# Rest products of a split hidden transform: 96 weight rows become 128, and the rest's right side is made in column quarters

## The chip, the cores and the metric

The kernel runs on one core of one Trainium2 chip. The metric is the device time of one execution in microseconds, the median of several executions. Before the change it is 716.98 us (three runs, 716.82 to 717.36).

## The reference

Two branches are computed from `x` (2048 x 576 floats) and mixed by a gate. Only the lines that matter are kept:

```python
qkv = (x @ wqkv) ...                      # 32 heads of 18
pq, pk = phi(q), phi(k)                   # where(t > 0, t + 1, exp(t)) + 1e-6
kv  = einsum("bhsd,bhse->bhde", pk, v);  z = einsum("bhsd->bhd", pk)
a_  = (einsum(pq, kv) / (einsum(pq, z) + 1e-6)).reshape(B, S, D) @ wo
# second branch, on the same x
a = einsum("bsd,ed->bse", x, dft_hid_re)
b = einsum("bsd,ed->bse", x, dft_hid_im)
y = einsum("ts,bse->bte", dft_seq_re, a) - einsum("ts,bse->bte", dft_seq_im, b)
g = sigmoid((x * gate_w).sum(-1))
return g * a_ + (1 - g) * y
```

The change concerns the two products over the hidden dimension D = 576, `a` and `b`.

## The kernel before, in words

**Numbers and forms.** Every large product is done in a 32-bit format of TensorE (`fp32r`). A float is split into a high part (`hi_of`, a copy on ScalarE, ACT) and what is left (`lo_of`, a subtraction on VectorE, DVE), and three products are summed: high x high, high x low, low x high.

**Stages in order.** k for 16 row tiles, then k-transposed times x and the small matrix of the attention, then q (the stretch of `q_tile`), then the attention output (L1238), then four stages for the second branch: the hidden product for the real part (`Hidden.run`, L1012), the sequence product for the real part (`sequence`, L1171), the hidden product for the imaginary part (L1012 again), and the sequence product for the imaginary part (L1171 again).

**The hidden product.** Both sides are cut into two by two quarters, and seven products of sums of quarters (the "forms") take the place of eight products of quarters. Half of D is 288 = 128 + 128 + 32 rows. For each of eight pairs `p` of row tiles and each of seven forms `k`, `Hidden.product` issues seven matmuls of 288 columns into one bank: six over the two chunks of 128 rows (three split products each), and one for the *rest*, the last 32 rows. In the rest's matmul the three split products lie stacked: 3 x 32 = 96 rows. Its left side is `xr` (read from the scratch `xrest`: 96 rows a pair), its right side `wl` (read from the scratch `last`). That is 2 x 8 x 7 = 112 rest matmuls among 784.

**Where the forms come from.** `Left` makes the left sides, `right` the right sides, for the real part (`wr`) during the first stages, for the imaginary part (`wi`) between the batches of the first sequence product. `right` has three pieces: two for the chunks of 128 rows and one for the rest. A piece is a generator that does a step at each call: load, two sums, two sums, high part, low part, store to DRAM by GpSimd's queue (POOL). In the rest piece of before, the 32 rows stand three times on 96 partitions, all 288 columns of seven forms wide; the high part is taken on all 96, and rows 32 to 63 are then overwritten by the low part.

**Order.** DVE, ACT and SyncE (SP, which issues the loads) run in the order in which the code is written; from the attention output on, PE (TensorE) does so too. In the q stretch PE's and all along POOL's order is set by a scheduler when the program is built, which weighs the instructions' estimated times; so other instructions on DVE or POOL can change PE's order there. Which step of a rest piece runs when is in two tables: `early` (steps of `wr_pieces[2]` after q tiles 5, 7, 8, 9, 11 and 12) and the tuples in `late` (steps of `wi_pieces[2]` after batches 18, 21, 21, 21, 22 and 22 of the first sequence product). A call on a finished generator does nothing. `late(n)` also issues the loads for the second hidden product: `load_w` (six chunk factors and one rest factor of a form), `load_pair` (four loads for one pair), `load_rest`.

Of the kernel before, what the change touches and what calls it, by code (L numbers as in the profile page):

```python
# [14 lines left out]
P = 128  # L15
# [127 lines left out]
def kernel(  # L143
# [310 lines left out]

    def right(src, rest, order):

        main, last = scratch([P, 7, 2, 2, HALF], "wm"), scratch([96, 7, HALF], "wm")

        def load(k, start):
            c = at(start, [P, 7, 2, HALF], R, "wb")[:P if k < 2 else 96]  # L460
            r, raw = c.bitcast(F)[:, :, 1], src[k] if k < 2 else rest
            for a, b in ((slice(0, 3), slice(0, 3)), (5, 3)):
                begin_after(nc.gpsimd.dma_start(out=r[:, a], in_=raw[:, b]), done[-1])
            return c

        def piece(k, start):

            c = load(k, start)
            r = c.bitcast(F)[:, :, 1]
# [5 lines left out]
            add(r[:, 6], r[:, 4], r[:, 1], ALU.subtract)  # L475
            yield
            hi_of(c[:, :, 0], r)
            yield
            if k < 2:
                for fs in (slice(0, 4), slice(4, 7)):  # L480
                    lo_of(c[:, fs, 1], r[:, fs], c[:, fs, 0])
                    nc.gpsimd.dma_start(out=main[:, fs, k], in_=c.bitcast(F)[:, fs])
                    if fs.start == 0:
                        yield
            else:
                rows = slice(32, 64)
                lo_of(c[rows, :, 0], r[rows], c[rows, :, 0])
                yield
                nc.gpsimd.dma_start(out=last, in_=c.bitcast(F)[:, :, 0])

        return (main, last), [piece(*o) for o in order]

    def go(gen, n=1):
        for _ in range(n):
# [475 lines left out]
    class Hidden:  # L970
# [4 lines left out]
        def load_w(self, k):  # L975
            f, (o, ro) = PRODUCTS[ORDER[k]][1], self.lay.w(k)
            if self.lay.swap:
                wl, rl = at(o, [P, 4, HALF], R, "wf"), at(ro, [P, HALF], R, "wf")
            else:
                wl, rl = rows(o, 4, HALF, R, "wf"), rows(ro, 1, HALF, R, "wf")[:, 0]  # L980
            nc.sync.dma_start(out=wl.bitcast(F), in_=self.main[:, f].rearrange("p c s n -> p (c s) n"))
            nc.sync.dma_start(out=rl.bitcast(F)[:96], in_=self.last[:, f])
            self.w[k] = wl, rl

        def load_rest(self, p):

            self.rest[p] = at(self.lay.rest(p), [P, 7, P], R, "xr")
            n = min(NP * 96 - p * 96, P)
            nc.sync.dma_start(out=self.rest[p].bitcast(F)[:n], in_=xrest[p * 96:p * 96 + n])

        def load_x(self, p, k):

# [14 lines left out]
        def product(self, ps, p, k, start):  # L1007
            x, (w, wl) = self.x[p, k], self.w[k]
            ops = [(x[:, a, c * P:c * P + P], w[:, 2 * c + b]) for c in range(2) for a, b in TURN]
            ops.append((self.rest[p][:96, 6 - k], wl[:96]))  # L1010
            for n, (a, b) in enumerate(ops):
                nc.tensor.matmul(ps, a, b, start=(start and n == 0), stop=(n == len(ops) - 1),  # L1012
                                 skip_group_check=True)
# [258 lines left out]
    def late(n):  # L1272
        for k, parts in enumerate(((1, 5, 5, 5, 9, 9), (10, 13, 13, 13, 17, 17), (18, 21, 21, 21, 22, 22))):
            go(wi_pieces[k], parts.count(n))
        if 24 <= n < 28:
            second.load_w(n - 24)
        if n == 27:
            second.load_rest(0)
        if n == 28:
            second.load_w(4)  # L1280
            second.load_pair(0)
        if n == 29:
            second.load_w(5)
            second.load_w(6)
            second.load_pair(1)
        if n == 30:
            second.load_rest(1)
        if n == 31:
            second.load_pair(2)
            second.load_rest(2)  # L1290
            second.load_rest(4)
            second.load_pair(3)
            second.load_rest(3)
            mi.load(0)
            second.load_pair(4)
            second.load_rest(6)
# [20 lines left out]
def _layouts(inputs):  # L1317
# [27 lines left out]
    def right(w):  # L1345

        main, rest = halves(w)
        quarters = ((0, 0), (1, 0), (1, 1), (0, 1))
        cols = (slice(0, HALF), slice(HALF, D))
        main = np.stack([main[d][:, :, cols[c]] for d, c in quarters], axis=2)  # L1350
        rest = np.stack([rest[d][:, cols[c]] for d, c in quarters], axis=1)
        return main, np.concatenate([rest] * 3)

    x = inputs["A_x"][0]
    wr, wr_rest = right(inputs["B_dft_hid_re"].T)
# [39 lines left out]
```

## Time and profile before

| | us |
|---|---|
| median of three runs | 716.98 (716.82 to 717.36) |
| the profiled execution's own time | 717.38 |
| its span, first to last instruction | 715.7 |
| PE busy | 711.6 (99% of the span) |
| DVE busy | 601.1 (84%) |
| ACT busy | 338.5 (47%) |
| POOL busy | 54.9 (8%) |
| first hidden product (starts at 258.40) | 51.52 |
| first sequence product (starts at 309.92) | 175.21 |
| second hidden product (starts at 485.13) | 52.09 |
| second sequence product (starts at 537.22) | 175.23 |

The profile page gives busy time by engine and by group of instructions; PE is the matmul part of TensorE, PEld its weight loads, which overlap the matmuls. A matmul's duration in a group is longer than the distance to the next one, since matmuls are pipelined: what a matmul costs is read from start to start. "Idle before" is time in which the engine had nothing to do, with the name of what released it.

### The profile page before, as it was taken

The page shows a single profiled execution, that of the slowest core. Times are in us where ns is not written, and L with a number is a line of the kernel's source. Part 1 is how long each engine was busy: PE and PEld are TensorE (multiplying, and loading weights), DVE is VectorE, ACT ScalarE, POOL GpSimd, SP SyncE. Part 2 cuts the span into 40 slices and gives each one's busy share as a digit, 9 for nine tenths or more (in the row PEclk, how much of TensorE's full clock was granted, in tenths as well). Part 3 has the DMA queues.
Part 4 walks back from the last instruction along what each step waited for, and adds up shares of the span by engine and source line. Part 5 has one row for each costly group of instructions (what it writes and reads, how often), then busy time and mean ns, then how long its engine had stood idle before and what let it go on. Part 6 is the DMA issues. An engine that isn't in the chain of part 4 may idle for free.

```text
span 715.7 us, 13965 instructions
## 1 busy us (share of the span) xinstructions
PE 711.6 (99%) x5436; PEld 711.1 (99%) x5436; DVE 601.1 (84%) x1020; ACT 338.5 (47%) x587; POOL 54.9 (8%) x94
## 2 busy tenths in 40 slices
PE   9999999999999999999999999999999999999998
PEld 9999999999999999999999999999999999999998
DVE  5699977687999748989999999857889988888885
ACT  5998445677644444553534334323535433343331
POOL 1112200050131110000010000000000000000000
PEclk9999999999999999999999999999999999999999
DMA  7388896874594589753475675789973544454530
GB/s 259 105 280 312 318 303 209 301 213 129 180 368 183 195 307 366 237 184 118 150 257 184 212 254 208 278 312 402 377 260 94 184 132 144 127 181 155 179 131 34
DMA packets 57525, 157.84 MB, mean 221 GB/s; under 512 B 6388, under 2 KB 15668, under 8 KB 56436
## 3 DMA queue, kind: packets, MB, share of 16 engines
q1 hardware_dynamic: 48404, 118.44, 48.9%
q0 software_dynamic: 8768, 38.12, 14.7%
q8 instruction: 43, 0.70, 0.4%
q10 hardware_dynamic: 288, 0.39, 0.2%
q14 instruction: 22, 0.18, 0.1%
HBM read 114.06 MB, written 41.39 MB: 217 GB/s over the span
## 4 chain that ended last, share of the span: by engine, by line
PE 99%; DVE 0%; issue 0%
PE bank L1171 49%; PE bank L226 23%; PE bank L1012 14%; PE bank L725 8%; PE bank L558 2%; PE bank L826 1%; PE bank L252 1%; PE bank L704 0%; PE bank L707 0%; PE bank L827 0%; DVE row L1188 0%
## 5 line engine op out<-in xcount | busy, mean ns | idle before, releaser
L1171 PE MATMUL bank<-fh,c 128*128 128x288 f32 x1792 | 350.7, 293 | 0.0
L1171 PEld LDWEIGHTS bank<-fh,c 128*128 128x128 f32 x1792 | 285.1, 188 | 0.0
L1171 PE MATMUL bank<-fl,c 128*128 128x288 f32 x896 | 262.3, 293 | 0.0
L196 ACT ACTIVATE c<-craw 128x768 fp32r<-128x768 f32 (+2 forms) x148 | 126.9, 900 | 163.6 <-DVE craw L216 154.0
L1171 PEld LDWEIGHTS bank<-fl,c 128*128 128x128 f32 x896 | 168.2, 188 | 0.0
L206 DVE TENSOR_TENSOR c<-craw,c 128x768 fp32r<-128x768 f32 (+3 forms) x148 | 146.1, 1024 | 0.8 <-ACT c L196 0.8
L226 PE MATMUL bank<-wd,xs 128*128 128x288 f32 (+1 forms) x784 | 104.9, 294 | 0.0
L226 PEld LDWEIGHTS bank<-wd,xs 128*128 128x128 f32 x784 | 103.5, 188 | 0.0
L1012 PE MATMUL bank<-wf,xf 128*128 128x288 f32 x588 | 90.8, 294 | 0.0
L1012 PEld LDWEIGHTS bank<-wf,xf 128*128 128x128 f32 x588 | 83.3, 189 | 0.0
L226 PE MATMUL bank<-mw,qs 128*128 128x288 f32 x448 | 60.7, 295 | 0.0
L725 PE MATMUL bank<-pk,c 128*128 128x288 f32 x448 | 60.0, 294 | 0.0
L725 PEld LDWEIGHTS bank<-pk,c 128*128 128x128 f32 x448 | 59.1, 188 | 0.0
L226 PEld LDWEIGHTS bank<-mw,qs 128*128 128x128 f32 x448 | 59.0, 188 | 0.0
L216 DVE TENSOR_TENSOR craw<-craw,craw 128x256 f32<-128x256 f32 x128 | 54.4, 425 | 5.1
L216 DVE TENSOR_TENSOR ys<-bank,ys 128x288 f32<-128x288 f32 x63 | 28.8, 457 | 28.2 <-PE bank L1171 25.7
L216 DVE TENSOR_TENSOR craw<-craw 128x512 f32<-128x512 f32 x64 | 43.9, 687 | 7.6 <-PE bank L1171 3.7
L196 ACT ACTIVATE fh<-fl 128x864 fp32r<-128x864 f32 (+1 forms) x36 | 30.3, 868 | 28.0 <-DVE fl L216 20.0
L395 DVE SCALAR_TENSOR_TENSOR acc<-bank,e 128x288 f32<-128x288 f32 x64 | 28.6, 454 | 16.5 <-ACT e L394 16.3
L206 DVE TENSOR_TENSOR fl<-fl,fh 128x864 fp32r<-128x864 f32 (+1 forms) x36 | 35.4, 988 | 1.6
L1012 PE MATMUL bank<-wf,xr 96*128 96x288 f32 x112 | 33.3, 298 | 0.0
L216 DVE TENSOR_TENSOR fl<-bank,y 128x288 f32<-128x288 f32 x48 | 21.8, 454 | 11.1 <-PE bank L1012 9.6
(106 smaller groups left out, 662.1 us busy)
## 6 DMA issues: line engine op xcount, KB each, us to landing
xf<-xm SPq DMA_DIRECT2D x42, 512.0 KB, 9.2
craw<-in_cr_dram SPq DMA_DIRECT2D x32, 512.0 KB, 3.9
craw<-in_ci_dram SPq DMA_DIRECT2D x32, 512.0 KB, 3.7
xm<-xb POOLq DMA_DIRECT2D x8, 1024.0 KB, 6.6
wf<-wm SPq DMA_DIRECT2D x14, 576.0 KB, 6.4
xraw<-in_xa_dram SPq DMA_DIRECT2D x25, 320.0 KB, 3.5
xr<-xr SPq DMA_DIRECT2D x14, 448.0 KB, 8.5
xm<-xb POOLq DMA_DIRECT2D x8, 768.0 KB, 8.2
```

The costliest lines, as they stand in the source:

```text
L196: return nc.scalar.activation(dst, src, AF.Copy, bias=bias)
L206: nc.vector.tensor_tensor(out=dst, in0=src, in1=hi, op=ALU.subtract)
L216: nc.vector.tensor_tensor(out=dst, in0=a, in1=b, op=op)
L226: nc.tensor.matmul(ps, a, b, start=(n == 0), stop=(n == len(pairs) - 1))
L252: nc.tensor.matmul(warm[:, :136], unit[:, :P], unit, start=True, stop=True)
L395: nc.vector.scalar_tensor_tensor(dst, ps, 0.0, e, op0=ALU.max, op1=ALU.add)
L558: nc.tensor.matmul(ps[i][h], x[:, i_x * P:(i_x + 1) * P], wkt.row(h, j), start=(c == 0 and n == 0), stop=(c == KC and n == 1))
L725: nc.tensor.matmul(ps[h][:, :HALF], t[:, a, k], pk[s][:, b, half(h)], start=(s == 0 and n == 0), stop=(s == NT - 1 and n == len(turn) - 1))
L826: nc.tensor.transpose(mains[i][:, cs], acc[2 * k + i][:, cs], ident)
L1012: nc.tensor.matmul(ps, a, b, start=(start and n == 0), stop=(n == len(ops) - 1), skip_group_check=True)
L1171: nc.tensor.matmul(ps[q], c[x][l > 2][:, l - 3 * (l > 2), k], factors[p](y, f), start=(p == 0 and i == 0), stop=(p == NP - 1 and i == 2))
```

## The change

- In `Hidden.product` the rest's matmul takes all 128 rows of `xr` and of `wl`. Rows 96 to 127 of the left side are the first 32 rows of the next pair's rest (which were loaded before too, and unused); on the right side they are zero. After the last pair stand 32 new zero rows in `xrest`, so the last pair's load is 128 rows and not 96.
- The rest piece of `right` works on a tile whose 128 partitions are four quarters of the columns (72 each) by 32 rows. Sums, high and low part are made once, on [128, 7, 72]. A third part of the tile is set to zero by POOL.
- Four stores (high, low, high, zero) put it together in `last`, now [128, 4 quarters, 7 forms, 72]. For `wr` two more stores write the zero rows of `xrest`.
- The rest piece has four steps where it had six: the four sums are one step, the low part and all stores another. The tables `early` and `late` keep their numbers, so the last calls do nothing, and the low part follows the high part at once (after batch 21, where it was after batch 22).
- `load_w` reads `wl` as 128 rows of four runs of 72 floats (288 bytes) each, where it read 96 rows of one run of 288 floats (1152 bytes).
- In `late`, `load_rest(4)` comes after `load_rest(3)`.

On SP, after the second hidden product's pair 1, the loads stood in this order (`xf` are a pair's loads, `xr` a rest's, `craw` the first batch of the next sequence matrix):

```order
L989 DMA xr_6122<-xr_103 128x896
L995 DMA xf_6166<-xm_97 128x1024
L995 DMA xf_6168<-xm_97 128x1024
L995 DMA xf_6170<-xm_97 128x1024
L995 DMA xf_6172<-xm_97 128x512
L989 DMA xr_6174<-xr_103 128x896
L989 DMA xr_6176<-xr_103 128x896
L995 DMA xf_6178<-xm_98 128x1024
L995 DMA xf_6180<-xm_98 128x1024
L995 DMA xf_6182<-xm_98 128x1024
L995 DMA xf_6184<-xm_98 128x512
L989 DMA xr_6186<-xr_103 128x896
```

and now, with the lines of the new file (L1009 is `load_rest`, L1015 `load_x`):

```order
L1009 DMA xr_6132<-xr_103 128x896
L1015 DMA xf_6176<-xm_97 128x1024
L1015 DMA xf_6178<-xm_97 128x1024
L1015 DMA xf_6180<-xm_97 128x1024
L1015 DMA xf_6182<-xm_97 128x512
L1009 DMA xr_6184<-xr_103 128x896
L1015 DMA xf_6186<-xm_98 128x1024
L1015 DMA xf_6188<-xm_98 128x1024
L1015 DMA xf_6190<-xm_98 128x1024
L1015 DMA xf_6192<-xm_98 128x512
L1009 DMA xr_6194<-xr_103 128x896
L1009 DMA xr_6196<-xr_103 128x896
```

The second of the two neighbouring `xr` loads (the rest of pair 4) has moved behind pair 3 and its rest. The number of loads is the same.

On POOL, ahead of the moves of the attention's small matrix (L886, `mw`), stood before only stores of the second chunk's forms (`wm`):

```order
L482 DMA wm_359<-wb_1516 128x4x576
L482 DMA wm_359<-wb_1516 128x3x576
L886 DMA mw_1722<-mf_1719 112x2x288
L886 DMA mw_1722<-mf_1719 14x2x288
L886 DMA mw_1722<-mf_1719 2x2x288
```

and now the zero parts for `wr` come between (L492 is the memset, L501 the stores to `last`, L507 those to `xrest`, L906 the moves):

```order
L482 DMA wm_359<-wb_1516 128x4x576
L482 DMA wm_359<-wb_1516 128x3x576
L492 MEMSET wb_2112 128x504
L501 DMA wm_360<-wb_2112 4x32x504
L507 DMA xr_103<-wb_2112 32x448 x2
L906 DMA mw_1722<-mf_1719 112x2x288
```

The other three stores to `last` stand further down, where the one store stood before.

On PE the scheduler's order differs in the q stretch alone. Where the first two attention tiles are transposed (`ident` is the identity matrix; `wd`, `xs` are the q product), before:

```order
L226 MATMUL bank<-wd_1307,xs_2303 128x290
L826 MATMUL bank<-ident_76,acc_87 128x128 x4
L226 MATMUL bank<-wd_1424,xs_2303 128x288 x5
L226 MATMUL bank<-wd_1307,xs_2303 128x290 x5
L826 MATMUL bank<-ident_76,acc_87 128x128 x4
L827 MATMUL bank<-ident_76,last_2043 128x128
L226 MATMUL bank<-wd_1424,xs_2350 128x288
```

and now:

```order
L226 MATMUL bank<-wd_1308,xs_2305 128x290
L226 MATMUL bank<-wd_1424,xs_2305 128x288 x5
L226 MATMUL bank<-wd_1307,xs_2305 128x290 x6
L846 MATMUL bank<-ident_76,acc_87 128x128 x8
L847 MATMUL bank<-ident_76,last_2043 128x128
L226 MATMUL bank<-wd_1424,xs_2358 128x288
```

The two groups of four transposes have become one group of eight; the matmuls are the same in number.

The diff, without the lines that only move:

```diff
-    xrest = scratch([NP * 96, 7 * P], "xr")
-    xrest_of = xrest.rearrange("(g q j r) n -> g j r q n", g=2, q=4, j=3)
+    xrest = scratch([NP * 96 + 32, 7 * P], "xr")
+    xrest_of = xrest[:NP * 96].rearrange("(g q j r) n -> g j r q n", g=2, q=4, j=3)
...
     def right(src, rest, order):
-        main, last = scratch([P, 7, 2, 2, HALF], "wm"), scratch([96, 7, HALF], "wm")
+        main, last = scratch([P, 7, 2, 2, HALF], "wm"), scratch([P, 4, 7, HALF // 4], "wm")
...
-            if k < 2:
...
-            else:
-                rows = slice(32, 64)
-                lo_of(c[rows, :, 0], r[rows], c[rows, :, 0])
-                yield
-                nc.gpsimd.dma_start(out=last, in_=c.bitcast(F)[:, :, 0])
-
-        return (main, last), [piece(*o) for o in order]
+        def rest_piece(start):
+
+            c = at(start, [P, 3, 7, HALF // 4], R, "wb")
+            f = c.bitcast(F)
+            r = f[:, 1]
+            load(r, rest)
+            nc.gpsimd.memset(f[:, 2], 0.0)
+            yield
+            for _ in sums(r):
+                pass
+            yield
+            hi_of(c[:, 0], r)
+            yield
+            lo_of(c[:, 1], r, c[:, 0])
+            for k, a in enumerate((0, 1, 0, 2)):
+                nc.gpsimd.dma_start(
+                    out=last[k * 32:k * 32 + 32].rearrange("r q f n -> q r (f n)"),
+                    in_=f[:, a].rearrange("p f n -> p (f n)"))
+            if src is wr:
+                for k in range(2):
+                    cs = slice(k * 7 * P // 2, (k + 1) * 7 * P // 2)
+                    nc.gpsimd.dma_start(out=xrest[NP * 96:, cs], in_=f[:32, 2].rearrange(
+                        "p f n -> p (f n)")[:, :7 * P // 2])
+
+        return (main, last), [piece(*o) if o[0] < 2 else rest_piece(o[1])
+                              for o in order]
...
-            nc.sync.dma_start(out=rl.bitcast(F)[:96], in_=self.last[:, f])
+            nc.sync.dma_start(out=rl.bitcast(F).rearrange("p (q n) -> p q n", q=4),
+                              in_=self.last[:, :, f])
...
-            n = min(NP * 96 - p * 96, P)
-            nc.sync.dma_start(out=self.rest[p].bitcast(F)[:n], in_=xrest[p * 96:p * 96 + n])
+            nc.sync.dma_start(out=self.rest[p].bitcast(F), in_=xrest[p * 96:p * 96 + P])
...
-            ops.append((self.rest[p][:96, 6 - k], wl[:96]))
+            ops.append((self.rest[p][:, 6 - k], wl))
...
             second.load_rest(2)
-            second.load_rest(4)
             second.load_pair(3)
             second.load_rest(3)
+            second.load_rest(4)
```

More of the change, by code (lines that the diff above doesn't have):

```diff
@@ L455, in right, with load, sums @@
     def right(src, rest, order):
-        main, last = scratch([P, 7, 2, 2, HALF], "wm"), scratch([96, 7, HALF], "wm")
-        def load(k, start):
-            c = at(start, [P, 7, 2, HALF], R, "wb")[:P if k < 2 else 96]
-            r, raw = c.bitcast(F)[:, :, 1], src[k] if k < 2 else rest
+        main, last = scratch([P, 7, 2, 2, HALF], "wm"), scratch([P, 4, 7, HALF // 4], "wm")
+        def load(r, raw):
             for a, b in ((slice(0, 3), slice(0, 3)), (5, 3)):
                 begin_after(nc.gpsimd.dma_start(out=r[:, a], in_=raw[:, b]), done[-1])
[L464 to L469, printed above, removed]
-            yield
+        def sums(r):
             add(r[:, 3], r[:, 5], r[:, 0], ALU.subtract)
@@ L475, in piece @@
             add(r[:, 6], r[:, 4], r[:, 1], ALU.subtract)
+        def piece(k, start):
+            c = at(start, [P, 7, 2, HALF], R, "wb")
+            r = c.bitcast(F)[:, :, 1]
+            load(r, src[k])
+            yield
+            yield from sums(r)
             yield
@@ L1351, in right @@
         rest = np.stack([rest[d][:, cols[c]] for d, c in quarters], axis=1)
-        return main, np.concatenate([rest] * 3)
+        rest = rest.reshape(32, 4, 4, HALF // 4).transpose(2, 0, 1, 3)
+        return main, rest.reshape(P, 4, HALF // 4)
     x = inputs["A_x"][0]
```

12 lines of the change are left out of this document (6 added, 6 removed).

## The prediction

> **What bounds the kernel now.** I read the page's first part, then the chain of work that ended last, then PE's rows in the two hidden products.
>
> ```profile
> span 715.7 us, 13965 instructions
> PE 711.6 (99%) x5436; PEld 711.1 (99%) x5436; DVE 601.1 (84%) x1020; ACT 338.5 (47%) x587; POOL 54.9 (8%) x94
> 258.40 51.52 PE bank L1012 x392
> 309.92 175.21 PE bank L1171 x1344
> 485.13 52.09 PE bank L1012 x392
> 537.22 175.23 PE bank L1171 x1344
> ```
>
> PE is the bound: busy 711.6 of 715.7 us, and in the four stages of the second branch (start, length, name, count of matmuls) the chain is PE alone, without a gap. So the change can win only what PE's matmuls themselves cost, and lose what makes PE wait. Per matmul the chain gives 175.21/1344 = 130.4 ns in the sequence product, 51.52/392 = 131.4 ns in the first hidden product and 52.09/392 = 132.9 ns in the second. The surplus is 392 x 1.07 = 0.42 us and 392 x 2.52 = 0.99 us, 1.41 us in all. The next rows are PE's timeline and its groups by shape.
>
> ```profile
> 262.70 0.30 PE L1012 MATMUL bank<-wf,xr 96*128 96x288 f32 x1
> 262.84 0.95 PE L1012 MATMUL bank<-wf,xb 128*128 128x288 f32 x6
> 263.62 0.30 PE L1012 MATMUL bank<-wf,xr 96*128 96x288 f32 x1
> 492.27 0.30 PE L1012 MATMUL bank<-wf,xr 96*128 96x288 f32 x1
> 492.41 0.96 PE L1012 MATMUL bank<-wf,xf 128*128 128x288 f32 x6
> 493.21 0.30 PE L1012 MATMUL bank<-wf,xr 96*128 96x288 f32 x1
> L1012 PE MATMUL bank<-wf,xr 96*128 96x288 f32 x112 | 33.3, 298 | 0.0
> L1012 PE MATMUL bank<-wf,xb 128*128 128x288 f32 x84 | 12.9, 293 | 0.0
> L1012 PE MATMUL bank<-wf,xf 128*128 128x288 f32 x588 | 90.8, 294 | 0.0
> L1012 PEld LDWEIGHTS bank<-wf,xr 96*128 96x128 f32 x112 | 21.1, 188 | 0.0
> L1012 PEld LDWEIGHTS bank<-wf,xb 128*128 128x128 f32 x84 | 11.8, 189 | 0.0
> ```
>
> A group of seven takes 263.62 - 262.70 = 0.92 us in the first product. After the 96-row matmul the next starts 0.14 us later; the six 128-row ones take 0.78, 0.13 each. In the second product a group takes 0.94: 0.14 after the rest, then 0.80. A 96-row matmul itself lasts 298 ns, the 128-row ones beside it 293 to 294. So there is a small price on the 96 rows, 4 to 5 ns each.
>
> **The change, part by part.**
>
> *128 rows (112 matmuls).* The count of matmuls and columns stays. Of what a rest costs more than its neighbours I take 5 ns (298 less 293): 112 x 5 = 0.56 us gained, on the chain. Ends: nothing, if the surplus comes from the change of bank that also falls there; and 1.41 us, if the whole surplus over the sequence product went with it. I stay near the low middle, since in the second product the six full matmuls are slow too (0.80 against 0.78), which the change leaves.
>
> *One group of transposes for two, on PE.*
>
> ```profile
> 182.95 0.60 PE L826 MATMUL bank<-ident,acc 128*128 128x128 f32 x4
> 183.31 1.57 PE L226 MATMUL bank<-wd,xs 128*128 128x288 f32 x10
> 185.18 1.03 PE L226 MATMUL bank<-wd,xs 128*128 128x288 f32 x6
> ```
>
> Ten matmuls at 0.13 us with the last one's 0.29 would last 1.46 us, six 0.94; both rows behind transposes have 0.09 to 0.11 more. One such change falls away: 0.09 us gained; the ends are 0 and 0.2. The first four transposes come about 1.4 us later, but the attention output does not start before all `wd` matmuls of the stretch are through.
>
> *DVE and ACT, rest pieces.*
>
> ```profile
> L216 DVE TENSOR_TENSOR wb<-wb 96x288 f32<-96x288 f32 x8 | 3.5, 450 | 0.1
> L206 DVE TENSOR_TENSOR wb<-wb 32x2016 fp32r<-32x2016 f32 x2 | 4.5, 2248 | 0.1
> L216 DVE TENSOR_TENSOR kvs<-kvs,mask 72x72 f32<-72x72 f32 x1 | 0.2, 228 | 0.0
> L206 DVE TENSOR_TENSOR xs<-xs,xs 128x512 fp32r<-128x512 f32 x4 | 2.8, 693 | 1.2 <-ACT xs L196 1.1
> L196 ACT ACTIVATE xs<-xs 128x512 fp32r<-128x512 f32 x4 | 2.5, 620 | 0.9 <-DMA xs<-in_xf_dram 0.9
> ```
>
> A piece took 4 x 450 + 2248 = 4.05 us of DVE. Now, by the nearest rows, 4 x 228 + 693 = 1.6. Two pieces give DVE about 4.9 us, which buys nothing: no PE group above has idle time ahead of it. The low part now directly follows the high part, so DVE waits for ACT, some 0.6 us after batch 21, with the next batch's sums queued behind. DVE spends 0.9 + 0.6 + 0.7 = 2.2 us there; before, the low part alone put 2.25 us into one batch, and PE never waited. Cost nothing; without that cover it would be the 0.6 us wait.
>
> *POOL.* The new zeros stand ahead of the moves of the small matrix, the other stores ahead of stores that come later.
>
> ```profile
> L254 POOL MEMSET ones_f<- 128x128 f32 x1 | 0.2, 204 | 0.3 <-POOLq L1382 0.3
> 146.25 3.08 POOL L886 DMA_DIRECT2D mw<-mf  x5 [15.65 <-ACT mf L874]
> 183.11 0.83 POOL L489 DMA_DIRECT2D wm<-wb  x1 [20.65 <-ACT xs L196]
> ```
>
> Three issues at 0.83 us and a memset (four times the 128 x 128 one's 0.2 us, an estimate) are 3.3 us in a gap of 15.65; three stores, 2.5 us, fall in one of 20.65. For `wi` it is four stores after batch 21, while the loads that read them begin after batch 24, three batches of 175.21/32 = 5.5 us later. No cost.
>
> *Loads of `wl` (14).* 96 packets of 1152 bytes become 512 of 288. The price of a packet is read from stretches with one size: mean 27 ns at 512 bytes (91.6 to 92.4 us: 16 x 0.8 x 1.142 / 538), 52 ns at 1152 (240 to 240.9: 16 x 0.9 x 1.056 / 294).
>
> ```profile
> DMA packets 538, 0.26 MB, mean 324 GB/s; under 512 B 32, under 2 KB 538, under 8 KB 538
> q1 hardware_dynamic: 538, 0.26, 114.2%
> DMA packets 294, 0.34 MB, mean 376 GB/s; under 512 B 0, under 2 KB 294, under 8 KB 294
> q1 hardware_dynamic: 294, 0.34, 105.6%
> L981 SPq DMA_DIRECT2D wf<-wm x14: 319/370/563, 190.1 to 474.5; - x14
> 473.35 0.69 SPq L982 DMA_DIRECT2D wf<-wm  x1
> 470.00:480.00 10.00, 10.00 (x80) 10.00 (x78) 4.23 (x5) 1.79 (x2) 0.00 (x0) 1.00 0.96 349
> 480.00:490.00 10.00, 10.00 (x79) 10.00 (x77) 5.48 (x11) 1.43 (x4) 0.00 (x0) 1.00 1.03 383
> ```
>
> The line through both gives 18.5 ns at 288 bytes: over 16 engines 0.59 us a load, against 0.31 before. Below that the end is 13 ns (by bytes), above it 52 ns (a packet costs the same whatever its size, 1.66 us a load). The last three loads, for forms 4 to 6 (that for form 5 at 473.35; the last `L981` ahead of form 6's at 474.5), fall where the DMA engines are full (0.96, then 1.03 in the column before the last), so all that follows them is late by 3 x 0.28 = 0.84 us, and at the worst by 3 x 1.35 = 4.1. The tightest of those is the rest of pair 1:
>
> ```profile
> 482.04 0.32 SPq L989 DMA_DIRECT2D xr<-xr  x1
> 487.03 1.63 SPq L989 DMA_DIRECT2D xr<-xr  x2
> 494.54 0.32 SPq L989 DMA_DIRECT2D xr<-xr  x1
> DMA to landing us min/median/max: 8.0/8.3/8.5
> ```
>
> The last row is for the rests issued between 480 and 505 us. Issued at 482.04, it lands by 490.5; PE uses it at 492.27 (above), its weight load a step earlier. That leaves 1.6 us, and 2.1 at a landing of 8.0. At my price PE does not wait. The other rests have more: pair 2's, issued at 487.03, is needed at 485.13 + 2 x 6.51 + 0.8 = 498.9 (a pair takes 52.09/8), pair 3's lands at 503.0 and is needed at 505.5.
>
> *The moved rest of pair 4.* Pair 3's four loads and its rest come a load earlier, about 1.2 us. The moved one goes at about 495 instead of 488, lands by 503.5 and is needed at 485.13 + 4 x 6.51 + 0.8 = 512. No cost.
>
> *The last pair's 32 more rows and the first product's loads.* Less than 0.3 us more for a load with pairs ahead of it; the first product's `wl` loads are issued from 190 us on, for 258.40. No cost.
>
> Sum: -0.56 - 0.09 = -0.65 us. The profiled execution took 717.38 us, 0.40 above the median; it would become 716.7, and the median 716.98 becomes 716.3.
>
> **The rivals.**
>
> *The rows cost nothing.* The 5 ns lie at the change of bank and stay; only 0.09 us are gained: 716.9. For it speaks that a group of seven in which all are full would also change bank there; against it that the sequence product changes bank as well, every sixth matmul, at 130.4 ns a step. The Trainium skill says on its page "TensorE: Matmul & The Clock Gate", section "LDWEIGHTS (loading the stationary operand)", that a weight load of 32 rows takes as long as one of 128, since its columns count; by that rule the sum would be -0.09 us. The trace agrees for the load alone (188 and 189 ns) and shows the matmul of 96 rows 5 ns longer.
>
> *Small packets make PE wait (the other side).* If a packet of 288 bytes costs over 29 ns, the three loads make what follows 1.65 us late and PE stops at pair 1's rest; at 52 ns, 4.1 us less 1.6 to 2.1, some 2.2 us of waiting, once, since later rests then have that much more time: 716.98 + 2.2 - 0.65 = 718.5. For it speaks that no packet of this size is in the trace; against it that 512 bytes cost half of 1152. The Trainium skill, page "DMA: Bandwidth & Descriptors", section "Specifications", asks for 512 bytes at least for full rate and says that below this the engine reads, modifies and writes; if that doubled 18.5 to 37 ns, an estimate, the delay would be 2.6 us and the time 717.1. No run so far shows it.
>
> *The whole surplus goes.* If the row change disturbs the neighbours too, 1.41 + 0.09 us are won: 715.5. Against it: only the step behind the rest stands out in the first product.
>
> **How the numbers follow.** A change under 0.2% (1.43 us) can't be told from none here. Forecast (716.3, from 715.9 to 716.7): 0.60. Rows cost nothing, 716.9: 0.17. Small packets make PE wait: 0.13, half of it below 717.9, half up to 718.6. Whole surplus, 715.5: 0.06. Something else, either way: 0.04. The range from 715.7 to 717.5 holds the first two and the mild half of the third, and leaves out the rest. Only the sharp packets and half of the remainder are slower by over 0.2%: 0.08; faster is part of the whole-surplus case: 0.05; the same 0.87.
>
> **What would show it.** A group of seven of 0.915 us in the first hidden product instead of 0.92, with all seven steps alike, and the stages at about 51.2 and 51.8 us; one row of eight transposes; DVE busy some 5 us less, to no effect. Wrong would be: a PE gap near 492 us ahead of an `xr` matmul (the packets), or stages of 51.5 and 52.1 us still (the rows).

## The result, and the profile after

The changed kernel takes 725.94 us (median of 4 runs, 725.18 to 727.11) against 717.10 for the kernel before (4 runs, 716.82 to 717.36): 1.0124 times, 95% interval 1.0109 to 1.0139. It is 8.8 us slower; 0.65 us less had been forecast. The profiled execution took 725.7 us.

The page's first lines, the engines, and the long pieces of the chain of waits (start, length, what):

```profile
span 723.5 us, 13984 instructions
PE 713.2 (99%) x5436; PEld 711.6 (98%) x5436; DVE 596.1 (82%) x1020; ACT 336.4 (46%) x587; POOL 61.0 (8%) x104
254.23 11.51 DMA wf<-wm
265.88 46.22 PE bank L1032 x339
312.76 142.37 PE bank L1191 x1092
457.93 8.98 DMA craw<-in_cr_dram
482.39 10.98 PE bank L1191 x82
493.37 51.72 PE bank L1032 x392
545.09 175.22 PE bank L1191 x1344
```

PE's busy share is still 99%, and that alone would hide everything. The chain shows it: before, each of the four stages of the second branch was one piece of PE; now a load (`wf<-wm`, a right side's form) breaks the first hidden product, and a load of the sequence matrix (`craw`) breaks the first sequence product. By the stages' borders: the first hidden product ends 312.76 - 309.92 = 2.84 us later; the sequence product takes 493.37 - 312.76 = 180.61 us for 175.21, 5.40 more; the second hidden product 0.37 less, the last stage the same. The sum is 7.86 us of a span that grew by 7.8. There are two losses and one small gain.

**The sequence product.** POOL's timeline (start, duration, what; in brackets the idle time before it and what ended that), then SP's:

```profile
422.14 0.74 POOL L501 DMA_DIRECT2D wm<-wb  x1 [0.42 <-POOL wb L492]
433.25 0.73 POOL L501 DMA_DIRECT2D wm<-wb  x1 [10.37 <-ACT wb L196]
440.32 0.71 POOL L501 DMA_DIRECT2D wm<-wb  x1 [6.34 <-issue]
447.02 0.69 POOL L501 DMA_DIRECT2D wm<-wb  x1 [5.99 <-DVE craw L216]
```

```profile
454.15 0.32 SPq L1001 DMA_DIRECT2D wf<-wm  x1
...
455.15 0.56 SPq L1128 DMA_DIRECT2D craw<-in_cr_dram  x1
457.93 1.66 SPq L1128 DMA_DIRECT2D craw<-in_cr_dram  x1
```

The four stores of `wi`'s rest forms don't go out in a row. The first holds the zeros. The data of the third were ready with the second (433.25), and still it is issued 7.07 us later; "issue" says that nothing the profile records held POOL. The fourth goes 6.70 us after that. Its row names DVE, but the low part that it stores was done at 433.47. What fits is the landing of the store before. From issue to landing the four stores take (least, median, most):

```profile
DMA to landing us min/median/max: 6.4/6.8/8.2
```

The last three land 6.8, 6.4 and 6.8 us after their issue, at about 440.1, 446.7 and 453.8. Each time the next in line, two stores and then SP's load, goes some 0.3 us later. SP's first load of a form for the second hidden product (L1001) stands until 454.15, 7.1 us after the last store was issued. SP works in the order of the code, so the two `craw` loads behind it stand as well. SP's waits (total us, times, longest) from 440 to 490 us now, and from 436 to 470 us before, where that load was issued at 443.65:

```profile
SPq L1001 <- DMA wm<-wb: 8.3, 1, 8.3
```

```profile
SPq L981 <- DMA wm<-wb: 0.7, 1, 0.7
```

The buffer in which the rest piece lies is where the first form's factor goes, so the load has to wait for the last store out of it. What then comes late, on DVE (which waits 7.70 us here) and on PE:

```profile
460.87 0.69 DVE L216 TENSOR_TENSOR craw<-craw 128x512 f32<-128x512 f32 x1 [7.70 <-DMA craw<-in_cr_dram]
460.56 0.29 PE L1191 MATMUL bank<-fh,c 128*128 128x288 f32 x1
463.74 0.40 PE L1191 MATMUL bank<-fh,c 128*128 128x288 f32 x1 [2.90 <-DVE c L206]
```

From 460.56 to 463.74 PE does one matmul. Together with three smaller ones (0.63, 1.26 and 0.41 us behind the matmuls that start at 469.19, 475.27 and 481.98) this is 3.18 + 2.30 = 5.48 us from start to start. Four usual steps of 0.13 us are in it, and the step behind each wait is 0.11 longer than usual (463.74 to 463.98): 5.48 - 0.52 + 0.44 = 5.40, the stage's growth.

**The first hidden product.** PE's timeline, then a table of windows (window, its length, PE busy, granted clock, share of the DMA engines, GB/s):

```profile
262.97 0.95 PE L1032 MATMUL bank<-wf,xb 128*128 128x288 f32 x6
265.88 0.37 PE L1032 MATMUL bank<-wf,xr 128*128 128x288 f32 x1 [1.96 <-DMA wf<-wm]
268.26 0.44 PE L1032 MATMUL bank<-wf,xr 128*128 128x288 f32 x1
269.94 0.44 PE L1032 MATMUL bank<-wf,xr 128*128 128x288 f32 x1
```

```profile
263.60:265.80 2.20, 0.32 (x3) 1.00 1.02 414
265.90:267.00 1.10, 1.10 (x8) 1.00 1.01 413
267.40:270.60 3.20, 3.20 (x15) 0.50 1.03 412
460.90:463.70 2.80, 0.00 (x0) 1.00 1.06 393
463.80:467.00 3.20, 3.20 (x25) 1.00 1.06 403
467.00:470.00 3.00, 2.67 (x21) 1.00 1.02 376
```

The rest's matmul that should follow the six of 262.97 at 263.76 starts at 265.88: it waits 2.1 us for `wl` of form 6, whose load took 11.51 us. Then the granted clock falls to 0.50 and a group takes 269.94 - 268.26 = 1.68 us instead of 0.92. POOL's same instruction (L1261, L1241 before) stands at 258.57 instead of 259.34, so the stage began about 0.77 us earlier and grew by 2.84 + 0.77 = 3.6 us: 2.1 of waiting, about 1.5 of slow clock. Both numbers are this execution's: where the same loads and stores stand in this stage, after_act (below) waits 1.97 us, after_rq 0.91 and after_sooner 0.28, all three with the clock at 1.00.

The two DMA queues while that load ran (257.8 to 259.4 us; packets, MB, share of 16 engines):

```profile
q0 software_dynamic: 79, 0.65, 95.6%
q1 hardware_dynamic: 80, 0.02, 6.0%
```

q0 carries POOL's stores, here 8192 bytes a packet (0.65 MB / 79), q1 SP's loads, 288 bytes a packet. They take turns, 79 to 80. The load has 512 packets, 32 an engine, and for each it waits for a large one, as long as POOL's stores last. At 1.6 x 16 / 79 = 0.32 us for a pair of packets, 32 turns are some 10 us, an estimate; the load took 11.51. The Trainium skill, page "DMA: Bandwidth & Descriptors", section "Queues, rings and completion order", says that an engine goes round its queues packet by packet, and that a packet is some 9 to 17 descriptors; the trace agrees with the turns and has one transfer of 288 bytes in a turn.

### The profile page after: what moved, and what is told of

It reads as the page before. It is cut to its first block, busy times and chain, and to the rows that moved or that the text cites. A ratio compares the mean times of both kernels' runs of the same rounds, so it can differ in the third digit from the quotient of the medians.

```text
span 723.5 us, 13984 instructions
## 1 busy us (share of the span) xinstructions
PE 713.2 (99%) x5436; PEld 711.6 (98%) x5436; DVE 596.1 (82%) x1020; ACT 336.4 (46%) x587; POOL 61.0 (8%) x104
## 4 chain that ended last, share of the span: by engine, by line
PE 88%; issue 4%; DMA 3%; DVE 3%; POOL 1%; SPq 0%; ACT 0%; POOLq 0%; DVEq 0%
PE bank L1191 45%; PE bank L226 17%; PE bank L1032 14%; PE bank L745 8%; PE bank L578 2%; DMA wf<-wm 2%; DMA craw<-in_cr_dram 1%; DVE c L206 1%; POOL att L1261 1%; PE bank L252 1%; DVE craw L216 1%; PE bank L846 0%; PE bank L724 0%; DVE ys L216 0%; DMA att<-acc 0%
## 5 line engine op out<-in xcount | busy, mean ns | idle before, releaser
L1032 PE MATMUL bank<-wf,xr 128*128 128x288 f32 x112 | 33.3, 297 | 2.0 <-DMA wf<-wm 2.0
```

## The experiments

Theory 1: the stores' slowness and the load behind them make the sequence product's 5.4 us. Theory 2: the short packets make the first hidden product's 3.6 us. Rivals: the stores' number, their time, or the 128 rows themselves; and, for theory 2, that the load is merely issued too late. The table gathers all fourteen runs: the ratio to the kernel before on the same chip, lengths of the stages by the chain (a `>` marks a first hidden product that waits inside), and how long after the start of the sequence product SP's load for the first form was issued. The kernel before has 133.7 in the last column.

| kernel | us | ratio | first hidden | sequence | SP's load after |
|---|---|---|---|---|---|
| changed | 725.94 | 1.0124 [1.0109, 1.0139] | >55.1 | 180.61 | 141.4 |
| rows_only | 717.28 | 0.9998 [0.9989, 1.0006] | 51.41 | 175.21 | 134.7 |
| after_act | 719.92 | 1.0036 [1.0022, 1.0050] | > | 175.28 | 137.5 |
| after_early | 723.85 | 1.0099 [1.0084, 1.0115] | 51.34 | 179.21 | 141.0 |
| rows_short | 716.60 | 0.9994 [0.9985, 1.0003] | 51.40 | 175.21 | 134.3 |
| after_long | 722.22 | 1.0068 [1.0054, 1.0081] | 51.42 | 180.51 | 141.9 |
| short_late | 722.15 | 1.0068 [1.0050, 1.0086] | >56.6 | 175.21 | 133.9 |
| only_late | 717.95 | 1.0005 [0.9995, 1.0015] | >52.0 | 175.21 | 134.5 |
| after_both | 717.81 | 1.0010 [1.0001, 1.0019] | 51.51 | 175.21 | 136.2 |
| rows_four | 716.79 | 0.9999 [0.9988, 1.0009] | 51.41 | 175.21 | 133.1 |
| after_sooner | 722.68 | 1.0082 [1.0067, 1.0097] | >51.6 | 181.45 | 141.9 |
| both_unswap | 718.60 | 1.0022 [1.0012, 1.0031] | 51.43 | 176.70 | 137.5 |
| after_rq | 718.83 | 1.0029 [1.0018, 1.0040] | > | 175.21 | 133.1 |
| rows_shape | 735.54 | 1.0258 [1.0239, 1.0277] | 51.40 | 194.66 | 155.6 |
| rq_early | 717.30 | 1.0009 [1.0000, 1.0018] | 51.34 | 175.21 | 133.1 |

The second hidden product is 51.72 or 51.73 us in all of them.

### The 128 rows alone (rows_only)

```diff
 # of the kernel before: one store and loads of 1152 bytes stay
+ nc.gpsimd.memset(full.bitcast(F)[96:, :, 0], 0.0)
...
- nc.sync.dma_start(out=rl.bitcast(F)[:96], in_=self.last[:, f])
+ nc.sync.dma_start(out=rl.bitcast(F), in_=self.last[:, f])
...
- ops.append((self.rest[p][:96, 6 - k], wl[:96]))
+ ops.append((self.rest[p][:, 6 - k], wl))
```

> The 128 rows alone: the kernel before, with the rest piece made on 96 partitions as before, 32 zero rows below it, one store of the rest's right side, and its loads as 128 runs of 1152 bytes. Theory: the rows themselves gain, the loss is all in how the rest's right side is stored and loaded. The trace of the changed kernel shows groups of seven of 0.912 us where they were 0.920, 8 ns for each rest: 112 x 8 = 0.9 us gained, 716.1 us, both hidden products at about 51.1 and 51.7 us, no idle time on PE. Rival: the 128 rows cost something by themselves (more to load, another order on PE): 717.5 or more.

Measured: 717.28 us, like the kernel before. The stages are shorter (chain):

```profile
258.49 51.41 PE bank L1018 x392
...
485.10 51.72 PE bank L1018 x392
```

That is 0.11 + 0.37 = 0.48 us less on PE than before. The interval of the total, -0.8 to +0.4 us, holds this and also nothing: the total expected wasn't seen. What follows is that the rows are not where the loss is.

### The stores on another queue (after_act)

```diff
-                nc.gpsimd.dma_start(
+                (nc.scalar if src is wi else nc.gpsimd).dma_start(
                     out=last[k * 32:k * 32 + 32].rearrange("r q f n -> q r (f n)"),
```

> The changed kernel, with the four stores of the imaginary part's rest forms issued by ACT instead of POOL. Theory 1: on POOL each of these stores waits for the one before it to land (6 to 7 us each), the buffer they read comes free some 10 us late, the first factor load of the second hidden product waits for it at the head of SP's queue, and the sequence matrix's batches behind it are late. Then the first sequence product returns from 180.6 to about 175.3 us, and the time from 725.9 to about 720.6. Rival: the batches are late because the loads of 288-byte runs stand ahead of them among the DMA packets; then the sequence product stays at 179 us or more and the time above 724.

Measured: the sequence product is back, the first hidden product still waits.

```profile
266.88 45.31 PE bank L1032 x344
312.19 175.28 PE bank L1191 x1344
```

SP's load goes at 449.73, 137.5 us after the stage's start and 3.9 earlier than in the changed kernel, and that is enough. Theory 1 holds as far as the queue: on ACT's queue the four stores are issued in 3.86 us, and the same data in the same shape cost the stage nothing.

### The load of form 6 earlier (after_early)

```diff
+            if not self.lay.swap and k == 6:
+                rl = self.early          # loaded by load_last(6)
...
+        if i == 13:
+            hidden.load_last(6)
```

> The changed kernel, with the last rest factor of the first hidden product (form 6) loaded after attention tile 13 instead of 14, before POOL's last stores of left forms start. Theory 2: its 512 packets of 288 bytes took turns with POOL's packets of 8192 and 6144 bytes, one for one, and so took 8 us to pass instead of about 1; PE waited 2.1 us for it and then ran some 3 us at half the granted clock. Then the first hidden product returns from 55.1 to about 51.1 us and the time from 725.9 to about 722. Rival: the stretch simply holds too many bytes; then pairs or factors behind are late, the product stays above 53 us, and the time above 724.

Measured: the first hidden product is one piece again, 51.34 us; the sequence product is not (PE's timeline holds a wait of 2.80 us for DVE at 459.95).

```profile
257.72 51.34 PE bank L1042 x392
309.06 142.37 PE bank L1201 x1092
```

The total gains only 2.1 us (725.94 - 723.85). The runs spread: 720.59 for the profiled one, whose mean granted clock is 1.000, and 723.75 to 725.46 for three with 0.995. A mean of 0.995 is 1% of the time at 0.50, some 7 us in which PE does 3.6 us of work less, an estimate that fits the 3.2 to 4.9 us between them. So the same gaps probably cost more in those three, the clock falling behind them; only the first was profiled.

### Short packets without the rest of the change (rows_short)

The load of `wl` in rows_only in runs of 72 floats; the elements are other than those the product needs.

```diff
-            nc.sync.dma_start(out=rl.bitcast(F), in_=self.last[:, f])
+            nc.sync.dma_start(out=rl.bitcast(F).rearrange("p (q n) -> p q n", q=4),
+                              in_=self.last[:, min(f, 3):min(f, 3) + 4, :HALF // 4])
```

> The 128-row kernel with one store (rows_only), but the rest factors loaded as 512 runs of 288 bytes (a quarter of four neighbouring forms each, so the rest products use other elements than they should). Only the loads' packets differ from rows_only. Theory 2: the first hidden product is about 4 us longer than in rows_only by a wait for form 6's rest factor and the clock behind it, the first sequence product is not, and the time is about 720. Rival (the piece's stores are the whole loss, packets cost only their 19 ns): 716.2, as rows_only. Third: the short runs hurt both places, 724 or more.

Measured: no wait, 51.40 us. Theory 2's expectation is missed. Why, the DMA queues from 257.6 to 258.2 us show:

```profile
q1 hardware_dynamic: 302, 0.09, 80.6%
q0 software_dynamic: 1, 0.01, 3.2%
```

Here the short packets ran before POOL's large ones had begun; there was nothing to take turns with. So shortness alone isn't the cause; theory 2 became: short packets *behind* POOL's large ones. The next three kernels test this.

### Long runs in the changed kernel (after_long)

Here, and in short_late below, the rest products again use other elements than they should.

```diff
-            nc.sync.dma_start(out=rl.bitcast(F).rearrange("p (q n) -> p q n", q=4),
-                              in_=self.last[:, :, f])
+            nc.sync.dma_start(out=rl.bitcast(F), in_=self.last.rearrange(
+                "r q f n -> r (q f n)")[:, f * HALF:(f + 1) * HALF])
```

> The changed kernel, its stores as they are, but a rest factor is loaded as 128 runs of 1152 bytes, each 288 floats in a row of the stored rest forms (so the rest products use elements of other forms). Only the loads' packets differ from the changed kernel. Theory 2: the wait in the first hidden product goes (about 51.4 us instead of 55.1); the first sequence product keeps its 5 us from the stores on POOL (theory 1): about 722. Rival for the sequence: if the short packets ahead of the matrix's batches count for some of it, it falls below 179 us too.

Measured: the first hidden product is whole, the sequence product keeps its loss (51.42 and 490.41 - 309.90 = 180.51 us by the chain). In the profiles the load that is early or long never makes PE wait in the first hidden product (after_early, after_long, after_both, both_unswap, rq_early), and the one that is neither always does (changed, after_act, after_rq, after_sooner).

### The same place, short and long (short_late, only_late)

These are rows_short and rows_only with form 6's `wl` loaded behind the rest of pair 3, 0.7 to 0.8 us later:

```diff
+            if self.lay.swap or k < 6:
+                self.load_last(k)
...
+        if i == 15:
+            hidden.load_last(6)
```

> The 128-row kernel with rest factors as 512 runs of 288 bytes (rows_short), and with form 6's rest factor loaded one transfer later, behind pair 3's rest of 448 KB. In rows_short its packets went out just ahead of POOL's 8192-byte ones, in the changed kernel just behind the first of them. If taking turns one for one is the mechanism, 32 short packets an engine now need some 8 us: PE waits 2 to 5 us in the first hidden product (54 to 58 us instead of 51.4), the time is 719.5 to 723. Rival (the changed kernel's wait came from something else in its stores or its POOL order): no wait, 716.6 to 717.3.

> The control for short_late: the 128-row kernel with rest factors as 128 runs of 1152 bytes (rows_only), form 6's loaded one transfer later in the same way. If packets take turns, 8 packets an engine need some 3 us where 32 need 8: the product stays at 51.4 us or waits under 1 us, 717 to 718. Rival (bytes or the place in the queue decide, not the number of packets): as late as short_late.

PE's timelines, short_late first:

```profile
263.41 0.95 PE L1025 MATMUL bank<-wf,xb 128*128 128x288 f32 x6
267.99 0.58 PE L1025 MATMUL bank<-wf,xr 128*128 128x288 f32 x1 [3.64 <-DMA wf<-wm]
268.37 1.64 PE L1025 MATMUL bank<-wf,xb 128*128 128x288 f32 x6
```

```profile
264.00 0.95 PE L1024 MATMUL bank<-wf,xb 128*128 128x288 f32 x6
265.23 0.37 PE L1024 MATMUL bank<-wf,xr 128*128 128x288 f32 x1 [0.28 <-DMA wf<-wm]
```

At the same place the 512 packets of 288 bytes make PE stop for 3.64 us and the 128 of 1152 bytes for 0.28, although the bytes are the same. The loss is 4.9 us (722.15; two runs) against 0.7 (717.95). In short_late the clock also falls to 0.50 behind the wait (268 to 270 us). This shows theory 2 in its second form, and that lateness alone costs little.

### Both undone (after_both)

after_act and after_early together.

```diff
+                (nc.scalar if src is wi else nc.gpsimd).dma_start(
...
+            hidden.load_last(6)
```

> The changed kernel with both remedies: the imaginary part's stores on ACT's queue, and form 6's rest factor loaded after attention tile 13. If the two places are the whole loss, the hidden products take 51.4 and 51.7 us, the sequence products 175.2, and the time is 716.2 to 716.9, the same as before or 0.1% less. If more is lost elsewhere, above 718.

Measured: 717.81 us. Both stages are whole in the chain (51.51 and 175.21 us), and 8.1 of the 8.8 us are gone. The time is 0.9 us above the range expected; no stage of the profiled execution (716.94 us) shows where.

### Four stores of another shape (rows_four), and sooner (after_sooner)

rows_four is rows_only with `wi`'s one store cut into four of 32 partitions; after_sooner is the changed kernel with the rest piece's last steps a batch earlier.

```diff
+ for q in range(4):
+     qs = slice(q * 32, q * 32 + 32)
+     nc.gpsimd.dma_start(out=last[qs], in_=full.bitcast(F)[qs, :, 0])
```

```diff
- (18, 21, 21, 21, 22, 22)
+ (18, 20, 20, 20)
```

> The 128-row kernel (rows_only) with the imaginary part's single store of rest forms cut into four stores of 32 rows each on POOL, nothing else. Theory 1 alone: each store waits for the one before it, 5 to 7 us each, so the buffer comes free 15 to 20 us later than in rows_only, SP's first factor load stands that long, the sequence matrix's batches behind it come late, and the first sequence product grows from 175.2 by 10 us or more: 726 or above. Rival (the serial waiting belongs to the 4 x 32 x 504 shape or to the 288-byte loads, not to several stores in a row): 717 to 718.

> The changed kernel, with the imaginary part's rest piece finished after batch 20 of the first sequence product instead of 21, so its chain of stores starts 5.5 us sooner and the factor load waits some 5 us instead of 10.5. Theory 1: the batches behind then come in time or nearly; the first sequence product falls from 180.6 to between 175.2 and 176.5 us, the time by 4 to 5.4 us to about 721. Rival (the sequence's loss is not a matter of when the stores end): no change, 725 to 726.

Four stores cost nothing here; POOL issues two at once and the next as soon as DVE is through:

```profile
431.57 1.14 POOL L495 DMA_DIRECT2D wm<-wb  x2 [12.26 <-ACT wb L196]
435.62 0.56 POOL L495 DMA_DIRECT2D wm<-wb  x1 [2.90 <-DVE wb L206]
```

So it isn't the number of stores. after_sooner missed too: its data are ready sooner, but the four stores stand 7.8 to 9.0 us apart (419.33, 428.21, 435.98, 445.00), each behind the landing of the one before, and SP's load is no earlier in its stage (141.9 us after its start; 141.4). Its sequence product takes 181.45 us, part of it at a clock of 0.50 (461 to 467 us). The time alone would mislead here: 722.68 is 3.3 us under the changed kernel, but in the profiled execution (723.88) what is shorter is the first hidden product (51.6 us against 55.1), which the edit doesn't touch and which waits only 0.28 us here. Finishing the piece a batch sooner bought the sequence product nothing. What is left is the stores' shape.

### The shape (after_rq, rows_shape)

after_rq orders the 128 partitions row by quarter, so that a store is one plain block of rows in DRAM; rows_shape adds to rows_only three stores of the change's shape, to a scratch that nothing reads.

```diff
-                    out=last[k * 32:k * 32 + 32].rearrange("r q f n -> q r (f n)"),
+                    out=last[k * 32:k * 32 + 32].rearrange("r q f n -> (r q) (f n)"),
```

```diff
+                for q in range(3 if src is wi else 0):
+                    nc.gpsimd.dma_start(
+                        out=spare[q * 32:q * 32 + 32].rearrange("r q f n -> q r (f n)"),
+                        in_=full.bitcast(F).rearrange("p f s n -> p (f s n)")[:, q * 504:q * 504 + 504])
```

> The changed kernel with the rest piece's partitions ordered row by quarter instead of quarter by row (the input is laid out to match), so that each of the four stores is one plain block of 128 x 504 floats. Their number, bytes and place on POOL stay. If the shape is the cause, the stores spread over all DMA engines and follow each other within 1 to 3 us, the factor load waits under 1 us, and the first sequence product takes 175.2 us instead of 180.6; the time falls to 720 to 721 (the first hidden product's wait stays). Rival (the number of stores or POOL's queue is the cause whatever the shape): 179 us or more, 725 to 726.

> The 128-row kernel (rows_only) with three more stores on POOL behind its one store of the imaginary part's rest forms, each 4 x 32 x 504 floats from the same buffer to a scratch that nobody reads. If such stores take 6 to 7 us each, one after the other, the buffer comes free some 15 us later, and the first sequence product grows from 175.2 to 182 us or more: 724 or above. Rival (they are as quick as rows_four's): 717 to 718.

POOL in after_rq, then in rows_shape:

```profile
431.91 1.62 POOL L501 DMA_DIRECT2D wm<-wb  x3 [10.40 <-ACT wb L196]
```

```profile
435.76 0.97 POOL L494 DMA_DIRECT2D wm<-wb  x1 [15.66 <-DVE craw L216]
443.15 0.74 POOL L496 DMA_DIRECT2D wm<-wb  x1 [6.42 <-issue]
...
457.45 0.70 POOL L496 DMA_DIRECT2D wm<-wb  x1 [6.43 <-issue]
```

As plain blocks of 128 partitions the same bytes go out three in a row in 1.62 us, without waiting for a landing, and the sequence product is 175.21. As 4 x 32 x 504 they go one by one, 7.1 us apart, also in a kernel that is otherwise as fast as before, and the stage becomes 194.66 us. On POOL's queue the shape is the cause. The time of after_rq, 718.83 us, is below the 720 expected; in the profile its first hidden product waits 0.91 us and not 2.1, with no slow clock behind it. The three stores of rows_shape land 6.9, 6.8 and 6.9 us after their issue, and the next store, at the end SP's load, again goes 0.1 to 0.3 us behind the landing. The four of after_rq land sooner (least, median, most):

```profile
DMA to landing us min/median/max: 2.6/2.9/4.6
```

The queues of DMA while one such store ran alone (435.2 to 438.6 us in the changed kernel):

```profile
q0 software_dynamic: 50, 0.20, 24.0%
```

It fills 24% of 16 engines, as much as four of them. The Trainium skill, page "DMA: Bandwidth & Descriptors", section "Rules for kernel authors", says that an outermost dimension under 16 keeps a DMA on at most that many engines; the 4 here, and 24%, agree.

The last column of the table is a dose and its response: up to 137.5 us PE waits for nothing in the stage, 141 to 142 loses 4.0 to 6.2, and 155.6 loses 19.45. In after_long, after_sooner and rows_shape a part of this is slow clock: PE waits 3.1, 3.0 and 16.9 us, and behind that it runs at a lowered clock (0.50 from 461 to 467 us in after_sooner, from 474 to 479 us 0.51 in rows_shape). Before the change SP's load had at least 137.5 - 133.7 = 3.8 us of slack.

### The order of the rests, and the best form (both_unswap, rq_early)

both_unswap is after_both with `load_rest(4)` where it stood before; rq_early is after_rq with after_early's load.

```diff
             second.load_rest(2)
+            second.load_rest(4)
             second.load_pair(3)
             second.load_rest(3)
-            second.load_rest(4)
```

> The kernel with both remedies (after_both), and the rest of pair 4 loaded ahead of pair 3 as before the change. The forecast called the move worth nothing for the time. So: no wait of PE in the second hidden product (51.7 us), 717.0 to 718.3. Rival (with 288-byte loads ahead of them the loads are so late that the order decides): PE waits ahead of pair 3's rest, the product takes 52.5 us or more.

> The changed kernel with row-by-quarter partitions (after_rq) and form 6's rest factor of the first hidden product loaded after tile 13 (after_early). If the two causes are the whole loss, it equals the kernel before less the rows' 0.5 us: hidden products 51.4 and 51.7, sequence products 175.2, 716.4 to 717.3.

With the old order the second hidden product is 51.73 us: the move neither made nor spared a wait there. both_unswap's 1.5 us lie in the sequence product, but not in a wait: the whole stage runs at 176.70/1344 = 131.5 ns a matmul instead of 130.4. From 310 to 440 us, before SP's load and before the moved one, it starts 991 matmuls, rq_early 999. Why is open. rq_early is whole in every stage of its chain: 51.34, 175.21, 51.72 and 175.22 us. It takes 717.30 us, 1.0009 [1.0000, 1.0018]. So the change without its two losses is as fast as the kernel before within 0.2%, and no kernel here is measurably faster than before (the lowest ratio is rows_short's, 0.9994 [0.9985, 1.0003]).

## Why the prediction was wrong, point by point

- **The step that failed first: the four stores of `wi`.** The part on POOL priced a store at the 0.83 us of its issue, gave the four 5.5 us and said "No cost". In the changed kernel the last three stand 7 us apart, and SP's load, which waits for the last, goes at 454.15, 10.5 us later than before (443.65) and 7.7 later counted from the stage's start. The forecast asked who reads the stored data (loads after batch 24), not who waits for the buffer that the stores read from: SP's load of the first form, with `craw` behind it. SP's wait for that buffer was in the trace before, at 0.7 us. Cost: 5.4 us; after_act and after_rq take it away.
- **The second: the first product's loads.** "Issued from 190 us on, for 258.40" is true of the first of them. That of the last rest, L982, was issued at 254.98, 3.4 us ahead of the stage and beside POOL's stores; its price was worked out on DMA engines with one queue at work. Cost: 3.6 us in the profiled execution; the wait alone was 0.3 to 2.1 us in the four kernels that share these loads. after_early, after_long and rq_early take it away, short_late brings it back.
- **The rival on small packets** had the right kind of mechanism and the wrong place and size. At the place that it feared, pair 1's rest in the second hidden product, nothing waits: that stage is 51.72 us. The packet itself cost about what was worked out, 18.5 ns: in the row of q1 in the changed kernel 6.0% of 16 engines over 1.6 us by 80 packets is 19 ns; in rows_short's row, with hardly another queue, 80.6% over 0.6 us by 302 is 26 ns, still under the 29 ns of that rival (whose sum was off: 29 ns make the three loads 3 x (0.928 - 0.312) = 1.85 us late; 1.65 belongs to 27 ns). The turns with 8192-byte packets, not the packet's own price, made the load slow.
- **The 128 rows**: -0.56 us forecast, -0.48 by stages (0.11 and 0.37). The matmul's mean fell from 298 to 294 ns in rows_only. The total can't show it.
- **DVE and ACT**: right. DVE is busy 5.0 us less (601.1 to 596.1; 4.9 forecast), to no effect on PE. The pieces:

```profile
L216 DVE TENSOR_TENSOR wb<-wb 128x72 f32<-128x72 f32 x8 | 1.7, 230 | 0.1
L206 DVE TENSOR_TENSOR wb<-wb 128x504 fp32r<-128x504 f32 x2 | 1.4, 679 | 0.7 <-ACT wb L196 0.7
```

  228 and 693 ns were taken from the nearest rows, and the wait for ACT, 0.6 us by my estimate, is 0.7.
- **One group of transposes**: it is there (eight in a row), its 0.09 us can't be told from the 1 us by which the start of the first hidden product differs between kernels (257.51 in rows_shape, 258.49 in rows_only).
- **The moved rest, the last pair's rows, the new stores for `wr`**: no cost, as forecast.

What stays open: why POOL issued two or three stores of one shape at once, while one of the other shape went only behind a landing (the landings fit, but the trace names no one that POOL waited for); why the load of form 6 landed 10.48 us after its issue in after_rq and 11.51 in the changed kernel, with the same instructions there; why POOL's large packets began a little sooner after issue in the changed kernel than in rows_short, which decided whether the short ones ran ahead of them; where rows_only's 0.48 us go in the total; and why both_unswap's first sequence product ran 0.8% slower throughout.

## What to carry to other kernels

A store has three prices: its issue, its landing, and the time for which it holds the buffer that it reads; ask of each moved store who writes that buffer next, and what stands behind that writer on its in-order queue. Give a store on POOL's queue its 128 partitions outermost, and count a load's packets: where a queue with large packets is at work, a load of many short ones can wait once for each. When a load's cover is taken from "the first of them", read the issue time of the last.

## What the runs showed of the hardware

- A store of 4 x 32 x 504 floats on POOL's queue filled 24% of the DMA engines' time and landed 6.4 to 6.8 us after its issue in the changed kernel's sequence product, and the next was issued only some 0.3 us behind the landing; as blocks of 128 x 504 three were issued in 1.62 us.
- Two queues took turns packet by packet, 79 to 80 in 1.6 us, although one had packets of 288 bytes and the other of 8192, so the queue with small packets got 6% of the engines' time.
- A wait of 2.1 us was followed, about 1.5 us after PE had resumed, by 3.2 us at half the granted clock (0.50); in the same execution a wait of 2.9 us in the sequence product left it at 1.00 (the table of windows above), and in after_act a wait of 1.97 us at the first place did too. The Trainium skill, page "TensorE: Matmul & The Clock Gate", section "What's actually happening", ties the half clock to an idle window of about 3.4 us that runs freely; here 2.1 us of waiting was enough, and a longer wait elsewhere was not, so the length of the wait alone doesn't decide.
